# Windowed attention and a feed-forward block: the exponential moved behind the transposition of the scores

## The chip, the cores and the metric

The program runs on one core of a Trainium2 chip. Five engines of that core matter here. PE (TensorE) multiplies matrices into PSUM, PEld is its loading of weights, DVE (VectorE) and ACT (ScalarE) do elementwise work out of PSUM and SBUF, and SP issues the DMAs. POOL (GpSimd) does almost nothing. The metric is the device time of one execution in microseconds, and less is better.

## The reference

Two blocks follow each other. The first is attention with a window, for 8 batches, 8 heads, 512 local rows, 32 global rows and a head width of 64.

```
k_all = concat(k_g, k_l);  v_all = concat(v_g, v_l)
out_g = softmax(scale * q_g @ k_all.T) @ v_all          # 32 global rows see everything
s_ll  = where(|i - j| <= 32, scale * q_l @ k_l.T, -1e9) # local rows see a window ...
s_l   = concat(scale * q_l @ k_g.T, s_ll)               # ... and the global rows
out_l = softmax(s_l) @ v_all
softmax(s): e = exp(s - max(s)); e / (sum(e) + 1e-9)
```

The second is a feed-forward block on all 4352 rows, with 512 columns in, 2048 hidden and 512 out: `h = x @ w_in`, `g = h * erf(softplus(h))`, `out = g @ w_out`.

## The kernel before

**Attention.** A head is one batch and one of 8 heads, so there are 64 of them. Heads come in pairs. For a pair, `scores` writes two PSUM tiles `s` (128 rows of queries, 4 tiles of them, 128 keys each). For a head, `mask_max` (DVE, four custom instructions) copies the scores to the SBUF tile `sm`, adds the mask and keeps each row's maximum in `mx`. What follows depends on the head. In the first 30 heads in the program's counting (`biased`, `BIASED = 30`) the function `exps` runs four ACTIVATEs of 128x128 on ACT, each `exp(maximum - x)` with `mx` as its bias. In the other 34 heads DVE subtracts the maximum from the whole tile in one instruction of 128x512, and ACT takes the exponential of the whole tile in one more. Then, for every head, PE transposes `sm` into the PSUM tile `t`, ACT or DVE copies `t` to the SBUF tile `pt`, PE multiplies `pt` with the values (`o`), and DVE or ACT divides by the row sum (`xn`). The sum of a row comes with the values, as a column of ones.

**Global rows.** Sixteen groups of four heads do the same for the 32 global rows. Their scores are the PSUM tiles `ga` and `gb`, the maximum is `gn`, ACT takes the exponential from PSUM into the SBUF tile `pg`, PE transposes `pg` in two halves, and ACT or DVE copies each half to `gt`. Of `pg` some columns stand between the written ones and are set once, to zero.

**Feed-forward.** Its work is laid between the heads from the start on. Products are written as three matmuls of high and low parts (`wh` and `wl`, `xh` and `xl`), `h` and `pa` to `pd` are the first product, `op` is the second. `gate` is one uninterrupted block on ACT, for up to three hidden tiles at a time while attention lasts: a table load for softplus, the softplus of the tiles, a table load for erf, the erf of the tiles, and a table load that brings the exponential back.

**Order.** Nothing is scheduled at run time. Each step is an `Op`, made by `add`, with the engines that may do it. The long string `ORDER` lists every step's number in the order in which the instructions are issued to the engines' queues, and an `a` behind a number says that ACT takes a step which DVE could do as well. A `w` in it is a filler: a matmul on constants into a spare bank. Each engine executes its queue in order, and a semaphore makes an instruction wait for the data and for free buffers. All DMAs are issued by SP, in the order of the string too. PSUM has 6 banks for attention and the second product, and 2 for `h`.

Most instructions pass through helpers, so their lines are the helpers' own: L374 is a matmul, L375 a transposition on PE, L376 an ACTIVATE, L377 a table load, L378 a DMA, L386 any DVE or POOL instruction.

Of the kernel before, what the change touches and what calls it, by code (L numbers as in the profile page):

```python
# [25 lines left out]
NENT = 24  # L26
MASK = -8.0e9
# [10 lines left out]
STEP, GKEY = 0.093, -1.339  # L38
# [99 lines left out]
w w w w w w w w w 4 349 w 348 352 314 315 316 2 321 0 3 363 1 317 318 377 364 404 376 53 353 354 323 322 324 444 445  # L138
334 335 55 446 325 361 59 336 380 326 54 337 327a 405 447 448 56 57a 381 449 450a 332 61 58 319 320 459 460 461 462
451 382 338a 29 350 487 391 31 383 452a 453 454 328 384a 329 330 333 339 340 60 392 463 379 5 30 355 356a 362 331 341  # L140
342a 32 33 408 409 419 455a 393 394a 343 344a 62 365 366a 345 432 351 389 346a 486 35 456 63 457a 458 6 378 390 410
420 367 368 64 357 358 359 34 435 436 360 437 417 464 465a 476 369 370 510 511 421 385 512 513 477 422a 466 467a 514
478 479a 395 37 433 386 406 499 438 549 396 387 388a 7 371 372a 439a 373 474 418 374a 397 407 489 468 490 36 398a 411
412a 517 38 515 516a 469 w 518a 470a 399 400a 500 501 525 434 39 40 423 552 401 8 424 402a 553 413 471 414 415 1364
472a 498 9a 10 554 416 425 426 440 441 442 551 563 11 475 488 41 491 473 443a 573 574 555 575 576 550 492 427 556a 577
428a 493a 13 430a 519 480 481 528 564 494 429 482 580 611 527 537 529 530 1365 483 495 578 539 502 496 520 42 12 588
620 503a 565 566a 1366a 521a 579a 497 43 375 484 1361 14 540 15 557 558 581a 504 44 505 559 560 506 522 523a 485 1362
526 16 45a 46 507a 541 542a 614 615 616 591 598 599 634 538 561 635 636 562 17 531 592 47 1363a 649 508 637 621 19
1355 1356 532a 509 638 622 18 543 533 534 582 589 1357a 567 48 623 590 600 583 535 536 1358 568 569 132 624a 596 570
601a 593 672 597 20 639 571 572 640a 619 617 1359 618a 49 612 1413 1360a 613 584a 544 594 595 652 545 546 659 1373 21  # L150
641 50 1370 642 585 586 587 547 548 653 695 696 654 602 643 603 606 644 604 1414 1367 605 645 733 697 607 608 698 699
660 1415 1371 675 682 683 646 647a 1416 710 655 656 651 700 676 673 347 702 1374 701a 703a 680 661 662 657 1368 658
625 1417 1418 736 756 1372a 51 1421 650 609 626 22 1377 627 1380 1375a 629 1378 1369a 677 737 757 610 1376 248 758
1419 1383 1422a 743 744 628 630 631 632 1387 65 1384 742 704 663 705 681 678 679a 706 1425 759 760 664 665 666a 648 52
66 1390 67 1426a 761 738 667 762a 713 714 684 633 720 735 68 707 708a 1427 715 794 739 716 797 1379 69a 668 669 23 70
403 25 670 685a 674 686 771 1420a 717a 431 687 690 24 763 688 721 1428a 718 689a 691 692a 740a 1423 712 26 798 27a 805
83 799 764 28 722 723a 806 807 774 775 819 820 1385a 745 800 741 746 1391a 821 709 822 823 719 1429 781 77 80 711 734
765 106 671 71 693 1388a 1424a 1381a 1386 766 767a 859 724 779 747 782 1382 748 749 750a 725 726 727 1389 795 801 524
# [177 lines left out]
def kernel(  # L336
# [120 lines left out]
    def attention(b, h, key):  # L457
# [37 lines left out]
        load(key - VLEAD, VB, vB[b, h], 333)  # L495
        st["va", h % 4] = VA

        biased = NH * b + h < BIASED
        if h % 2 == 0:
            st["s"] = SS = [psum_a([P, 4, P], f"s_{nm}_{i}") for i in range(2)]  # L500

# [1043 lines left out]
```

## Time and profile before

| what | value |
|---|---|
| median of 3 runs | 889.73 us |
| lowest and highest run | 883.45 and 890.32 us |
| the profiled execution's own time | 886.39 us |
| its span, first to last instruction | 884.6 us |
| granted TensorE clock, mean | 0.998 |
| PE busy | 865.7 us, 98% of the span |
| DVE busy | 685.2 us, 77% |
| ACT busy | 566.7 us, 64% |
| DMA queue of the program | 185.02 MB, 64.9% of 16 engines' span |

The span lies 1.8 us below that execution's own time. The shares of busy time are averages over a program whose stages differ: attention with feed-forward work between the heads until about 325 us, then feed-forward work alone. So the same numbers are taken by stretches further down. The ends of matmuls are modelled, so a busy PE says that matmuls follow each other, and the time from one start to the next says how fast.

### The profile page before, as it was taken

The page shows a single profiled execution, that of the slowest core. Times are in us where ns is not written, and L with a number is a line of the kernel's source. Part 1 is how long each engine was busy: PE and PEld are TensorE (multiplying, and loading weights), DVE is VectorE, ACT ScalarE, POOL GpSimd, SP SyncE. Part 2 cuts the span into 40 slices and gives each one's busy share as a digit, 9 for nine tenths or more (in the row PEclk, how much of TensorE's full clock was granted, in tenths as well). Part 3 has the DMA queues.
Part 4 walks back from the last instruction along what each step waited for, and adds up shares of the span by engine and source line. Part 5 has one row for each costly group of instructions (what it writes and reads, how often), then busy time and mean ns, then how long its engine had stood idle before and what let it go on. Part 6 is the DMA issues. An engine that isn't in the chain of part 4 may idle for free.

```text
span 884.6 us, 22103 instructions
## 1 busy us (share of the span) xinstructions
PE 865.7 (98%) x8752; PEld 711.6 (80%) x8753; DVE 685.2 (77%) x1810; ACT 566.7 (64%) x1025; POOL 0.9 (0%) x5
## 2 busy tenths in 40 slices
PE   6899999999999999999999999999999999999998
PEld 4678787888888888888888888888888888888986
DVE  5989998999998989899988977496647956355443
ACT  6989989766766866775746845565644653465660
POOL 0000000000000000000000000000000000000000
PEclk9999999999999999999999999999999999999999
DMA  9889998988788766887776529343573536335212
GB/s 331 298 276 322 311 293 294 308 271 279 253 267 267 237 219 200 282 284 256 233 243 206 175 83 328 101 131 120 156 248 96 163 101 193 117 112 149 86 69 71
DMA packets 120062, 186.42 MB, mean 211 GB/s; under 512 B 14104, under 2 KB 57624, under 8 KB 119960
## 3 DMA queue, kind: packets, MB, share of 16 engines
q1 hardware_dynamic: 119960, 185.02, 64.9%
q8 instruction: 69, 1.13, 0.5%
q14 instruction: 33, 0.27, 0.1%
HBM read 143.56 MB, written 41.42 MB: 209 GB/s over the span
## 4 chain that ended last, share of the span: by engine, by line
PE 90%; DVE 4%; DMA 4%; ACT 1%; issue 1%; SPq 0%; DVEq 0%
PE op L374 40%; PE h L374 11%; PE pd L374 7%; PE pa L374 7%; PE pc L374 7%; PE pb L374 4%; PE o L374 3%; PE s L374 3%; PE t L375 3%; PE h_g L374 2%; PE go L374 1%; PE ga L374 1%; PE gt L375 1%; DVE sm L386 1%; DMA raw_in<-in_w_in_dram 1%; DVE top_in L386 1%
## 5 line engine op out<-in xcount | busy, mean ns | idle before, releaser
L374 PE MATMUL op<-wouth,gh 128*128 128x512 f32 x544 | 214.7, 395 | 0.1
L374 PE MATMUL op<-wouth,gl 128*128 128x512 f32 x544 | 212.0, 390 | 0.0
L374 PE MATMUL op<-woutl,gh 128*128 128x512 f32 x544 | 211.8, 389 | 0.0
L377 ACT ACT_TABLE_LOAD x105 | 134.7, 1283 | 2.5 <-PEq L1532 0.7
L374 PEld LDWEIGHTS op<-wouth,gl 128*128 128x128 f32 x544 | 102.1, 188 | 21.5
L374 PEld LDWEIGHTS op<-wouth,gh 128*128 128x128 f32 x544 | 102.2, 188 | 20.5 <-ACT xg L376 0.3
L374 PEld LDWEIGHTS op<-woutl,gh 128*128 128x128 f32 x544 | 102.3, 188 | 20.0
L376 ACT ACTIVATE gh<-sp 128x512 fp32r<-128x512 f32 x75 | 46.9, 629 | 96.2 <-PE op L374 87.3
L386 DVE TENSOR_TENSOR gl<-sp,gh 128x512 fp32r<-128x512 f32 x136 | 91.7, 687 | 20.3 <-PE op L374 16.0
L376 ACT ACTIVATE sp<-sp 128x512 f32<-128x512 f32 x136 | 76.0, 621 | 0.5
L386 DVE CUSTOM_DVE_ANT_0 sm<-s,msk 128x128 f32<-128x128 f32 x256 | 58.3, 285 | 14.0 <-ACT msk L376 7.0
L374 PE MATMUL h<-xh,winh 128*128 128x512 f32 (+1 forms) x168 | 66.4, 395 | 0.0
L386 DVE CAST gh<-sp 128x512 fp32r<-128x512 f32 x61 | 25.6, 420 | 50.6 <-PE op L374 50.3
L374 PE MATMUL pa<-xh_x_B,wq 128*128 128x512 f32 x184 | 64.1, 389 | 0.0
L374 PE MATMUL pd<-xh_ih_T,wq 128*128 128x512 f32 x184 | 64.0, 389 | 0.0
L374 PE MATMUL h<-xh,winl 128*128 128x512 f32 (+1 forms) x168 | 63.3, 377 | 0.0
L374 PE MATMUL h<-xl,winh 128*128 128x512 f32 (+1 forms) x168 | 63.0, 375 | 0.0
L386 DVE TENSOR_TENSOR pair<-u,pc 128x512 f32<-128x512 f32 x46 | 31.4, 684 | 25.3 <-PE pc L374 25.1
L374 PEld LDWEIGHTS pd<-xh_ih_T,wq 128*128 128x128 f32 x184 | 34.5, 188 | 7.5 <-ACT abs_l_in L376 0.2
L374 PEld LDWEIGHTS pa<-xh_x_B,wq 128*128 128x128 f32 x184 | 34.5, 188 | 7.2
L375 PE MATMUL t<-cs,sm 128*128 128x128 f32 x256 | 39.1, 279 | 0.5 <-DVE mx L386 0.5
L376 ACT ACTIVATE sm<-sm,mx 128x128 f32<-128x128 f32 x120 | 37.6, 399 | 2.8 <-DVE mx L386 2.8
(158 smaller groups left out, 1685.7 us busy)
## 6 DMA issues: line engine op xcount, KB each, us to landing
wq<-wq SPq DMA_DIRECT2D x161, 256.0 KB, 3.5
vb<-in_vB_dram SPq DMA_DIRECT2D x64, 325.0 KB, 5.3
qk<-in_qk_dram SPq DMA_DIRECT2D x28, 656.0 KB, 6.2
rx<-xsc SPq DMA_DIRECT2D x26, 512.0 KB, 6.5
va<-in_vA_dram SPq DMA_DIRECT2D x64, 195.0 KB, 4.8
wq<-part SPq DMA_DIRECT2D x47, 256.0 KB, 4.0
part<-os SPq DMA_DIRECT2D x34, 256.0 KB, 3.8
os<-part SPq DMA_DIRECT2D x34, 256.0 KB, 3.9
```

What stands on the lines that cost most here:

```text
L374: pe = lambda n, *a, **k: pinned(nc.tensor.matmul(n, *a, **k))
L375: tr = lambda *a, **k: pinned(nc.tensor.transpose(*a, **k))
L376: act = lambda *a, **k: pinned(nc.scalar.activation(*a, **k))
L377: table = lambda name: pinned(nc.scalar.preload_act_table_set(name))
L386: return lambda *a, **k: pinned(f(*a, **k))
```

## The change

The exponential leaves its place ahead of the transposition. Ahead of it only the maximum is subtracted, on DVE (one instruction of 128x512) or on ACT (four of 128x128, with the function Identity), as `ORDER` says for each head. The copy of the transposed tile out of PSUM becomes the exponential, so it is now always on ACT. The global rows are treated in the same way, and the untouched columns of `pg` are set to -1e30 in place of zero, so that their exponential is zero. `mx` has 6 buffers in place of 2. `ORDER` is another list.

```diff
@@ ORDER is another list of step numbers; its first line before:
-w w w w w w w w w 4 349 w 348 352 314 315 316 2 321 0 3 363 1 317 318 377 364 404 376 53 353 354 323 322 324 444 445
...
-    add({"POOL": 0.7}, -99, lambda: pool.memset(PG.ap, 0.0), writes=[PG])
+    add({"POOL": 0.7}, -99, lambda: pool.memset(PG.ap, LOWEST), writes=[PG])
...
-        MX = abuf([P, 4], f"mx_{nm}", "mx", 2)
+        MX = abuf([P, 4], f"mx_{nm}", "mx", 6)
...
         def mask_max(ts=range(4)):
+            biased = shift.eng == "ACT"
...
-        def exps():
+        def subtract(e):
+            if e == "DVE":
+                dve.tensor_tensor(SM.ap, SM.ap, MX.ap.unsqueeze(2).to_broadcast([P, 4, P]), ALU.subtract)
+                return
             for t in range(4):
-                act(SM.ap[:, t, :], SM.ap[:, t, :], AF.Exp, bias=MX.ap[:, t : t + 1], scale=-1.0)
+                act(SM.ap[:, t, :], SM.ap[:, t, :], AF.Identity, bias=MX.ap[:, t : t + 1], scale=-1.0)
...
-        if biased:
-            add({"ACT": 1.18}, key, exps, [TAB, MX] + ([PIECE[3, h]] if NH * b + h < 2 else []), [SM])
-        else:
-            add({"DVE": 0.62, "POOL": 1.13},
-                key,
-                lambda e: vec[e].tensor_tensor(
-                    SM.ap, SM.ap, MX.ap.unsqueeze(2).to_broadcast([P, 4, P]), ALU.subtract
-                ),
-                [MX],
-                [SM],
-            )
-            add({"ACT": 0.55}, key, lambda: act(SM.ap, SM.ap, AF.Exp, scale=scale), [TAB], [SM])
+            shift = add({"DVE": 0.62, "ACT": 1.18}, key, subtract, [MX], [SM])
...
-        add({"ACT": 0.52, "DVE": 0.61}, key + STEP * 2, lambda e: copy(e, PT.ap, T.ap), [T], [PT])
+        add(
+            {"ACT": 0.55},
+            key + STEP * 2,
+            lambda: act(PT.ap, T.ap, AF.Exp, scale=scale if shift.eng == "DVE" else 1.0),
+            [T, TAB],
+            [PT],
+        )
...
-            act(body, GA.ap.rearrange("p (m x) -> p m x", x=96), AF.Exp, bias=NM.ap, scale=scale)
-            act(PG.ap[:, 672:736], GB.ap, AF.Exp, bias=NM.ap, scale=scale)
-
-        add({"ACT": 0.8}, key, exps, [GA, GB, NM, TAB], [PG])
+            for dst, src in ((body, GA.ap.rearrange("p (m x) -> p m x", x=96)), (PG.ap[:, 672:736], GB.ap)):
+                if e == "DVE":
+                    dve.tensor_scalar(dst, src, scale, NM.ap, op0=ALU.mult, op1=ALU.add)
+                else:
+                    act(dst, src, AF.Identity, bias=NM.ap, scale=scale)
+
+        add({"DVE": 0.74, "ACT": 0.8}, key, subtract, [GA, GB, NM], [PG])
...
-                {"ACT": 0.42, "DVE": 0.48},
+                {"ACT": 0.44},
                 key + STEP * 2,
-                lambda e, T=T, m0=m0: copy(e, GT.ap[:, m0 : m0 + 3, :], T.ap),
-                [T],
+                lambda T=T, m0=m0: act(GT.ap[:, m0 : m0 + 3, :], T.ap, AF.Exp),
+                [T, TAB],
                 [GT],
```

Counted over the whole program, the change moves instructions as follows. The 34 ACTIVATEs of 128x512 on `sm` are gone. The ACTIVATEs of 128x128 on `sm` go from 120 to 156 (30 heads to 39), the DVE subtractions from 34 to 25. Writing `pt` goes from 50 on ACT and 14 on DVE to 64 on ACT, writing `gt` from 24 on ACT and 8 on DVE to 32 on ACT. Writing `pg` goes from 16 groups on ACT to 9 on ACT and 7 on DVE. Table loads stay at 105. Among the first 30 heads, counted by batch and head, six have the subtraction on DVE after the change (none before), and five had their `pt` written by DVE before (none after). Fillers go from 11 to 4: ten of the 11 stand ahead of PE's first score, and the 4 stand in the first batches' heads.

What ACT issues around the end of batch 4 and the start of batch 5 before, where each head's number follows its tile (`sm_4_7` is batch 4, head 7):

```order
L376 ACTIVATE sm_5_3_3899<-sm_5_3_3899 128x512
L376 ACTIVATE sm_4_7_3612<-sm_4_7_3612 128x512
L376 ACTIVATE pg_78<-ga_5_0_3947,gn_5_0_4007 128x5x96
L376 ACTIVATE pg_78<-gb_5_0_3948,gn_5_0_4007 128x64
L376 ACTIVATE sm_5_0_3986<-sm_5_0_3986 128x512
L376 ACTIVATE pt_4_7_4059<-t_4_7_4058 128x512
L376 ACTIVATE os_0_1_1_4070<-op_0_1_1_3973 128x512
L376 ACTIVATE part_3_2_4075<-top_l_in_3_1_3798 128x256
L376 ACTIVATE hs_0_2_3_4113<-h_0_2_3_3811 128x512
L376 ACTIVATE os_0_1_0_4168<-op_0_1_0_4077 128x512
L376 ACTIVATE part_3_5_4172<-top_l_in_3_0_3387 128x256
L376 ACTIVATE pt_5_0_4096<-t_5_0_4095 128x512
```

What ACT issues there in the changed kernel:

```order
L375 ACTIVATE sm_5_0_3828<-sm_5_0_3828,mx_5_0_3829 128x128 x4
L375 ACTIVATE gh_0_1_5_3926<-sp_0_1_5_3282 128x512
L376 ACT_TABLE_LOAD
L375 ACTIVATE sp_0_2_0_4006<-hs_0_2_0_3582 128x512
L375 ACTIVATE sp_0_2_1_4007<-hs_0_2_1_3542 128x512
L375 ACTIVATE sp_0_2_2_4008<-hs_0_2_2_3594 128x512
L376 ACT_TABLE_LOAD
L375 ACTIVATE sp_0_2_0_4006<-sp_0_2_0_4006 128x512
L375 ACTIVATE sp_0_2_1_4007<-sp_0_2_1_4007 128x512
L375 ACTIVATE sp_0_2_2_4008<-sp_0_2_2_4008 128x512
L376 ACT_TABLE_LOAD
L375 ACTIVATE pt_5_0_4028<-t_5_0_4027 128x512
```

Before, head 5_0 passes ACT twice, for its exponential (`sm_5_0`) and for the write of `pt_5_0`. In the changed kernel it passes ACT for the subtraction and then for the write of `pt_5_0`, which is the exponential; between the two stands a whole gate block, whose last instruction brings back the table for the exponential.

What DVE issues at the start before, from the `mask_max` of the last of the first four heads on, where `top_in` is the conversion of a tile of weights and `gm`, `gn` are maxima of the global rows:

```order
L386 ISA sm_0_1_245,mx_0_1_246<-s_0_0_1_161,msk_76 128x128
L386 ISA mx_0_1_246 128x1
L386 TENSOR_SCALAR top_in_0_2_0_251<-raw_in_0_2_0_199 128x512
L386 SCALAR_TENSOR_TENSOR top_in_0_2_0_251<-raw_in_0_2_0_199,top_in_0_2_0_251 128x512 x2
L386 TENSOR_REDUCE gm_0_0_243<-gb_0_0_234 128x1
L386 TENSOR_SCALAR gn_0_0_319<-gm_0_0_243 128x1
L386 SCALAR_TENSOR_TENSOR top_in_0_2_0_251<-winh_0_2_308,top_in_0_2_0_251 128x512
L386 ISA sm_0_4_325,mx_0_4_326<-s_0_4_0_268,msk_76 128x128
L386 ISA mx_0_4_326 128x1
```

What DVE issues first of all in the changed kernel:

```order
L385 TENSOR_SCALAR top_in_0_2_0_117<-raw_in_0_2_0_106 128x512
L385 SCALAR_TENSOR_TENSOR top_in_0_2_0_117<-raw_in_0_2_0_106,top_in_0_2_0_117 128x512 x2
L385 SCALAR_TENSOR_TENSOR top_in_0_2_0_117<-winh_0_2_111,top_in_0_2_0_117 128x512
L385 ISA sm_0_2_185,mx_0_2_186<-s_0_2_0_151,msk_76 128x128
L385 ISA mx_0_2_186 128x1
```

The conversion of the first tile of weights (four instructions on `top_in_0_2_0`) moves from behind the `mask_max` of four heads to the very start.

What SP issues first before, where `q` and `k` are queries and keys of a pair of heads (`0_2` is batch 0, heads 2 and 3), `mby` is the mask and `raw_in` a tile of weights:

```order
L378 DMA k_0_2_116<-in_qk_dram 128x768
L378 DMA q_0_2_119<-in_qk_dram 128x544
L378 DMA q_0_0_155<-in_qk_dram 128x288
L378 DMA k_0_0_156<-in_qk_dram 128x416
L378 DMA mby_77<-in_cst_dram 128x128
L378 DMA cs_75<-in_cst_dram 128x194
L378 DMA q_0_0_155<-in_qk_dram 128x256
L378 DMA k_0_0_156<-in_qk_dram 128x352
L378 DMA k_0_4_189<-in_qk_dram 128x768
L378 DMA q_0_6_195<-in_qk_dram 128x544
L378 DMA q_0_4_197<-in_qk_dram 128x544
L378 DMA raw_in_0_2_0_199<-in_w_in_dram 128x512
```

What SP issues first in the changed kernel:

```order
L377 DMA raw_in_0_2_0_106<-in_w_in_dram 128x512
L377 DMA k_0_0_110<-in_qk_dram 128x416
L377 DMA q_0_2_114<-in_qk_dram 128x544
L377 DMA mby_77<-in_cst_dram 128x128
L377 DMA q_0_0_109<-in_qk_dram 128x288
L377 DMA k_0_2_125<-in_qk_dram 128x768
L377 DMA cs_75<-in_cst_dram 128x194
L377 DMA k_0_0_110<-in_qk_dram 128x352
L377 DMA vb_0_1_129<-in_vB_dram 128x650
L377 DMA va_0_6_131<-in_vA_dram 128x390
L377 DMA q_0_0_109<-in_qk_dram 128x256
L377 DMA k_0_4_226<-in_qk_dram 128x768
```

The weights go from the 12th place to the first, the mask stays about where it is, the second half of `q_0_0` goes from 7th to 11th, and the keys of the pair 0_2 from 1st to 6th.

## Rows read from the trace of the kernel before

**Rows 1.** The page: the span, and PE's busy time, share and instructions.

```profile
span 884.6 us, 22103 instructions
PE 865.7 (98%) x8752; PEld 711.6 (80%) x8753; DVE 685.2 (77%) x1810; ACT 566.7 (64%) x1025; POOL 0.9 (0%) x5
```

**Rows 2.** Busy us of each engine by stretches, granted clock, DMA share, GB/s.

```profile
0.00:5.00 5.00, 4.23 (x14) 1.38 (x14) 0.00 (x0) 1.28 (x1) 0.94 (x5) 1.00 0.65 193
5.00:18.00 13.00, 6.55 (x228) 4.54 (x231) 8.15 (x48) 8.45 (x24) 0.00 (x0) 1.00 1.01 363
18.00:22.00 4.00, 4.00 (x91) 3.24 (x87) 3.91 (x15) 3.71 (x11) 0.00 (x0) 0.57 1.06 395
22.00:110.00 88.00, 80.50 (x1985) 63.50 (x1975) 80.40 (x348) 79.86 (x209) 0.00 (x0) 1.00 0.90 301
110.00:143.00 33.00, 32.90 (x693) 27.05 (x693) 30.06 (x100) 28.88 (x64) 0.00 (x0) 1.00 0.97 322
143.00:331.00 188.00, 187.70 (x3270) 153.24 (x3259) 173.09 (x627) 134.97 (x262) 0.00 (x0) 1.00 0.81 260
331.00:862.00 531.00, 531.00 (x2434) 443.43 (x2433) 382.59 (x663) 308.95 (x459) 0.00 (x0) 1.00 0.55 172
...
```

**Rows 3.** PE's waits, longest first: what waited, for whom, us, times, longest.

```profile
PE s L374 <- issue: 2.8, 2, 2.0
PE s L374 <- DVE mx L386: 2.4, 1, 2.4
PE gt L375 <- ACT pg L376: 2.1, 1, 2.1
PE s L374 <- DMA q<-in_qk_dram: 1.9, 1, 1.9
PE ga L374 <- DMA qk<-in_qk_dram: 1.6, 1, 1.6
...
```

**Rows 4.** PE's waits from 143 us to the end, all of them.

```profile
PE t L375 <- DVE mx L386: 0.3, 1, 0.3
```

**Rows 5.** Instructions on `sm`: ns min/median/max, first and last start, shapes.

```profile
L376 ACT ACTIVATE sm<-sm,mx x120: 384/394/453, 7.4 to 129.7; 128x128 f32<-128x128 f32 x120
L386 DVE TENSOR_TENSOR sm<-sm,mx x34: 650/685/694, 116.3 to 310.7; 128x512 f32<-128x512 f32 x34
L376 ACT ACTIVATE sm<-sm x34: 613/630/720, 118.7 to 322.9; 128x512 f32<-128x512 f32 x34
```

**Rows 6.** Groups by line: busy us, mean ns of one | idle before.

```profile
L377 ACT ACT_TABLE_LOAD x105 | 134.7, 1283 | 2.5 <-PEq L1532 0.7
L376 ACT ACTIVATE sp<-sp 128x512 f32<-128x512 f32 x136 | 76.0, 621 | 0.5
...
L376 ACT ACTIVATE sm<-sm,mx 128x128 f32<-128x128 f32 x120 | 37.6, 399 | 2.8 <-DVE mx L386 2.8
L376 ACT ACTIVATE pt<-t 128x512 f32<-128x512 f32 x50 | 29.7, 602 | 10.3 <-PE t L375 10.3
...
L376 ACT ACTIVATE pg<-ga,gn 128x480 f32<-128x480 f32 x16 | 10.6, 661 | 8.9 <-DVE gn L386 8.0 <-PE go L374 0.9
...
L386 DVE TENSOR_REDUCE gm<-ga 128x1 f32<-128x480 f32 x16 | 10.4, 652 | 0.6 <-PE ga L374 0.6
...
L386 DVE COPY pt<-t 128x512 f32<-128x512 f32 x14 | 9.6, 684 | 0.3
```

**Rows 7.** The start, by time: start us, us, instruction, [idle before].

```profile
0.77 4.27 PE L374 MATMUL spare<-const-bfloat16-1.0 128*128 128x512 bf16 x10 [0.77 <-PEq L1532]
...
4.97 1.95 PE L374 MATMUL s<-k,q 64*32 64x128 f32 x96
...
6.37 0.63 ACT L376 ACTIVATE msk<-mby 128x512 f32<-128x512 uint8 x1 [4.36 <-DMA mby<-in_cst_dram]
...
13.94 0.43 DVE L386 TENSOR_SCALAR top_in<-raw_in 128x512 int32<-128x512 int32 x1 [1.62 <-DMA raw_in<-in_w_in_dram]
14.40 1.42 DVE L386 SCALAR_TENSOR_TENSOR top_in<-raw_in,top_in 128x512 int32<-128x512 int32 x2
```

More of the change, by code (lines that the diff above doesn't have):

```diff
@@ L26 @@
 NENT = 24
+LOWEST = -1.0e30
 MASK = -8.0e9
@@ L143 @@
[L143 to L152, printed above, removed]
@@ new lines @@
+2040a 2167 1731 1991 1994 1990 1732a 2041 2000 1997 1992 1733 1911 2001a 1998 1742 1735 1916 2168 1737 1921 1738 1739
+1926 2002 1741 1743 2169 2004 1999 2042 2003 1744 1748 2006 2020 2074 2082 2090 2008 2005 2007 1912 1745 2009 1747
+2188 2043 1917 1913a 2189 2172 2044a 1922 1914 1749 2173 1750a 1927 1751 2010 2045 2046 2012 2047a 2011 2190 1918a
+2048 2021 2013 2191 1919 2049 2023 2022 2192 2170 2027 2024 2193 2171 2025 2194 2098 2028 1752 2174 2029 2209 2026
+2175 2031 2210 2030 2179a 2195 2211 2050 2181a 2053 2033 2212 2051 2196a 2056 2054a 2052 2069 2213 2183a 2055 2059
@@ new lines @@
+2432 2153 2433 2161 2434 2287 2442 2301a 2289 2307 2440a 2467 2310 2304a 2313 2452 2468 2438a 2316 2288 2138 2453a
+2469 2290 2435 2146 2140 2291 2148 2439 2141 2326 2443a 2470 2149 2292 2441 2154 2444 2334 2331 2156 2162 2302 2339
+2305 2157 2342 2308 2319 2164 2309 2454 2311 2165 2312 2350 2455 2471 2347 2456 2314 2315 2317 2458 2355 2457a 2320
+2472 2318 2327 2323 2487 2358 2335 2343 2351 2460 2321 2322 2324 2473 2488 2325 2359 2328 2474a 2489 2362 2365 2336
+2459 2368 2344 2461 2462 2464 2463 2490 2352 2465 2491 2475 2360 2363a 2361 2477 2364 2492 2476 2371 2479 2478 2493
@@ L263 @@
+3004 2904 3012 3005 3013 3007 2916 3015 3008 2924 3016 2932 2909 2917 2911 2925 2919 2912 2933 2927 2920 2935 2928
+2937 2936 2938
 """
@@ L564, in attention @@
             add({"DVE": 0.44}, key + 0.001, lambda: mask_max(range(2, 4)), [S, MSK, PIECE[2, 0], SM, MX], [PIECE.setdefault((3, h), fixed(None))])
+            shift = add({"DVE": 0.62, "ACT": 1.18}, key, subtract, [MX, PIECE[3, h]], [SM])
         else:
             add({"DVE": 0.86}, key, mask_max, [S, MSK], [SM, MX])
-        if biased:
-            add({"ACT": 1.18}, key, exps, [TAB, MX] + ([PIECE[3, h]] if NH * b + h < 2 else []), [SM])
-        else:
-            add({"DVE": 0.62, "POOL": 1.13},
-                key,
-                lambda e: vec[e].tensor_tensor(
-                    SM.ap, SM.ap, MX.ap.unsqueeze(2).to_broadcast([P, 4, P]), ALU.subtract
-                ),
-                [MX],
-                [SM],
-            )
-            add({"ACT": 0.55}, key, lambda: act(SM.ap, SM.ap, AF.Exp, scale=scale), [TAB], [SM])
+            shift = add({"DVE": 0.62, "ACT": 1.18}, key, subtract, [MX], [SM])
         T = psum_a([P, 4, P], f"t_{nm}")
```

228 lines of the change are left out of this document (112 added, 116 removed).

## The prediction

> **What bounds the kernel now.** I read the page's busy shares first, then the table of stretches, then PE's waits, then single groups. PE is busy for 865.7 of 884.6 us [rows 1], which leaves 18.9 us of idle time in the whole span. The reader is to see where it lies [rows 2]. From 143 to 862 us PE idles for 0.3 us (188.0 less 187.7, then 531.0 of 531.0), and its list of waits from 143 us to the end has one entry of 0.3 us [rows 4]. That its busy time there is real work is seen in the rate: 2434 matmuls in 531 us are one in 0.218 us, nearly all of 512 columns, which is the higher clock level of 2.4 GHz with little between them. Nothing that ACT or DVE saves there can end sooner, unless PE gets fewer instructions, and this change gives it none fewer but fillers. The idle time is early: 6.45 us in 5 to 18 us (13.00 less 6.55), 7.5 us in 22 to 110 us, 0.1 us in 110 to 143 us. In that early part all are loaded: from 22 to 110 us DVE is busy for 80.4, ACT for 79.9 of 88 us, and the DMA engines at 0.90 [rows 2]. The longest waits of PE there have five different causes [rows 3].
>
> **The removed pass.** The 34 heads that passed both DVE and ACT ahead of the transposition, and then ACT or DVE once more, lose one pass. Their instructions start at 116.3 us at the earliest and go on to 322.9 us [rows 5]. On ACT, 34 of 0.630 us go (-21.4). The 36 more pieces of 128x128 cost 37.6/120 = 0.313 us each of busy time (+11.3), the 14 more writes of `pt` cost 29.7/50 = 0.594 (+8.3), and the 7 fewer writes of `pg` save 10.6/16 = 0.66 (-4.6) [rows 5, 6]. That is -6.4 us. On DVE 9 subtractions of 0.685 (-6.2) and 14 copies of 9.6/14 = 0.686 (-9.6) go. The 7 writes of `pg` come: no row shows that instruction, the nearest is the maximum over the same PSUM tile, 0.65 us (+4.6) [rows 5, 6]. That is -11.2 us. In all some 17.6 us of two engines, nearly all behind 116 us, where the work that hides it is PE's own: PE idled 0.4 us from 110 to 331 us. **Worth: 0 us** (at best -0.4).
>
> **The other heads.** In the first 30 heads nothing is removed. Four ACTIVATEs of 128x128 with `mx` as bias stay four of that shape and bias, with another function. The copy out of PSUM becomes an exponential out of PSUM. No row has one of 128x512. Its bounds are the copy from PSUM (0.594 us) and the exponential from SBUF (0.630), 0.04 us apart, or 2.3 us of ACT over 64 heads. I take the copy's, since both read PSUM. What differs early is who does it. Six subtractions go from ACT (4 x 0.313 = 1.25) to DVE (0.685): ACT -7.5, DVE +4.1. Five writes of `pt` go from DVE to ACT: DVE -3.4, ACT +3.0. Three of the first seven `pg` go to DVE: ACT -2.0, DVE +2.0. So ACT gets 6.5 us less and DVE 2.7 us more, on some 110 us. Of the 7.5 us that PE idles in 22 to 110 us, 2.8 are charged to "issue" and 1.6 to the DMA of `qk` [rows 3], neither of which the change touches. The other 3.1 us are waits on ACT or DVE. The ends are -3.1 us (all gone) and +2.7 us (DVE's added work passed on to PE whole). I take **-1.0 us**, a third of the gain, since ACT is relieved by more than DVE is loaded, but DVE is the fuller of the two.
>
> **The start.** Rows give the pace of the loads. PE's first scores start at 4.97 us, once 384 + 272 KB are in (a column of 128 rows is 0.5 KB), and the mask's conversion at 6.37 us, 416 KB later [rows 7]. That is 297 KB per us. In the new order of SP the mask is behind 1056 KB in place of 1072, so no later. But the keys for the first `mask_max` now end at 1584 KB, 4.97 + 928/297 = 8.1 us. Their 64 matmuls take 1.3 us (96 took 1.95), so DVE's first `mask_max` starts near 9.4 in place of 7.0 us (+2.4). Against this DVE has the conversion of weights done by then, 0.43 + 1.42 + half of 1.42 for the last = 2.6 us (-2.6), which formerly came at 13.94 us after a wait of 1.62 us for its load, and that wait goes (-1.6). A new wait comes: the second half of `q_0_0` is 11th in SP's queue, at 2505 KB, 4.97 + 1849/297 = 11.2 us. With its scores done at 11.8 us, DVE waits for about 0.6 us from 11.2, when two heads' worth at 0.9 are done (+0.6). In sum **-1.2 us**, between -6.4 (PE's waits of 2.4, 2.1 and 1.9 us all gone) and +2.4 (the later scores felt in full).
>
> **The fillers.** Ten stood in the wait for the first load, so their 4.27 us [rows 7] are worth nothing by themselves. What they do is seen by the clock: each took 427 ns for 512 columns, the level of 1.2 GHz, and the scores behind them ran at the level of 2.4 (granted 1.00 from 5 to 18 us). Then, after 13 us in which PE was busy for only 6.55, the granted clock was 0.57 in 18 to 22 us [rows 2], which cost 4.0 x 0.43 = 1.7 us of work. Without fillers PE enters the first scores cold. The ends are 0 (the lower level lies in the waits, 6.45 us of them from 5 to 18 us) and +6.5 us (all of the 6.55 us of work takes twice as long, and nothing hides it). I take **+1.7 us**, the price of the one stretch at the lower level that the trace has. The Trainium skill, page "TensorE: Matmul & The Clock Gate", section "What's actually happening", says that the throttled clock is the default and that activity releases it, which speaks against taking the fillers out; by it alone the sum would be nearer the upper end, 890.7 us. The trace agrees, with 427 ns in the first fillers and 0.57 after the idle stretch. The four fillers that stand later cost 0.218 us each at most (+0.9); they stand among the first batches' heads, where PE idles anyway, so I count 0.
>
> **The sum.** 886.39 us, the profiled execution's own time, -1.2 - 1.0 + 1.7 = **885.9 us**. That execution lies 3.3 us below the median of 889.73 and inside the runs' 883.45 to 890.32. So 885.9 may be seen as no change, and the next median may as well lie some 3 us to either side of it. About 1% is what a measurement of this kernel tells from no change: 880.8 and 898.6 us.
>
> **Rivals.**
> *Faster: the early idle time closes.* The new list of steps is free to rearrange everything, and ACT has 6.5 us less to do before 116 us. Should PE's 7.5 us of 22 to 110 us and the stretch at the lower clock (1.7) both go, the time is 886.4 - 9.2 = 877.2 us. For it speaks that DVE and ACT are at 91% there, so that little relief shortens queues. Against it: "issue" and the DMA hold 4.4 us of it, the DMA engines are at 0.90 to 1.06 until 143 us, and DVE gets more, not less. Chance 0.15.
> *Cold start.* The lower clock lasts through the first scores and is not hidden: +6.5 - 1.2 - 1.0 on 886.4, or 890.7 us, up to 893 if the start's gain fails too. For: the fillers are gone. Against: idle time of nearly the same size to hide it. Chance 0.12.
> *Slower: the exponential sits behind a gate block.* Only ACT can now empty the bank `t`. A block is three table loads of 1.283 us and six passes of 76.0/136 = 0.559 us, 7.2 us [rows 6], uninterrupted, and the order on ACT shows one right between the subtraction and the exponential of head 5_0. Where PE's queue has less than 7.2 us of other work between a head's transpositions and its values, PE waits with everything behind it, in the stretch that has no waits now. It decides from two blocks on (of 105/3 = 35) that catch PE for their whole length: 886.4 + 14.4 = 900.8 us. Against: 50 of 64 writes of `pt` were on ACT already, behind the same blocks, and PE waited 0.3 us in all from 143 us on [rows 4]. Chance 0.07.
>
> **How the numbers follow.** The forecast, no change, has 0.66, and its own range is 881 to 891 us: the ends of the early heads (-3.1, +2.7) and of the start, not all on one side, and the runs' scatter. The range that should hold 8 in 10 reaches into the cold start (893) and into the faster case (879). Left out are two thirds of the faster case, 0.10, the gate blocks, 0.07, and 0.03 of the rest. Faster by over 1% (under 880.8 us): 0.13, nearly all of the faster case. Slower by over 1%: 0.07, the gate blocks. Within 1%: 0.80.
>
> **What would show it.** The removed pass: ACT's 34 instructions of 128x512 on `sm` are gone, DVE's busy share of 143 to 331 us falls from 173.1 us by about 10, and PE's idle time there stays under 1 us. The early heads: PE's idle time of 22 to 110 us stays between 5 and 10 us. The start: DVE's first instruction is the conversion at about 4.5 us, its first `mask_max` comes at 9 to 10 us. The fillers: the clock shows a longer stretch at the lower level before 25 us. Gate blocks: a wait of PE's `o` on ACT's `pt` of several us. I am wrong if PE idles for more than 20 or less than 7 us behind 5 us, or if its matmuls of 331 to 862 us take another time each, for which I know no reason.

## The result: 1.1% slower, nearly all of it lost before 331 us

The changed kernel takes 899.4 us (median of 6 runs, 893.17 to 901.11) beside 889.73 us for the kernel before (6 runs, 883.45 to 891.05), a ratio of 1.0110 [1.0075, 1.0145]. Measured once more later, it came to 898.63 us and 1.0129 [1.0085, 1.0172]. That is not the "no change" of the forecast. The profiled execution took 901.11 us with a span of 899.3. It is the slowest of its six, and that of the kernel before (886.39 us) lies below its median, so the two traces are 14.7 us apart and the medians 9.7.

The page of the changed kernel, to be read beside [rows 1]: PE is busy for 871.4 us. Before it was 865.7, or 861.4 without the ten fillers at the start, so 10.0 us more go into the same work and three more late fillers, and 4.7 us more into idle time (27.9 in place of 18.9 + 4.3).

```profile
span 899.3 us, 22044 instructions
...
PE 871.4 (97%) x8743; PEld 717.2 (80%) x8746; DVE 679.5 (76%) x1804; ACT 560.9 (62%) x1019; POOL 0.9 (0%) x5
```

The table of stretches of the changed kernel, with the columns of [rows 2]:

```profile
0.00:5.00 5.00, 0.00 (x0) 0.00 (x0) 0.96 (x2) 1.96 (x2) 0.94 (x5) 1.00 0.63 214
5.00:18.00 13.00, 9.15 (x217) 6.34 (x218) 6.90 (x40) 4.32 (x12) 0.00 (x0) 1.00 1.02 363
18.00:22.00 4.00, 3.99 (x93) 3.06 (x94) 3.93 (x20) 3.92 (x12) 0.00 (x0) 1.00 1.00 317
22.00:110.00 88.00, 75.78 (x1780) 60.57 (x1780) 73.30 (x316) 67.28 (x177) 0.00 (x0) 0.92 0.80 260
110.00:143.00 33.00, 32.52 (x676) 27.03 (x673) 31.65 (x120) 29.19 (x67) 0.00 (x0) 1.00 0.91 297
143.00:331.00 188.00, 185.50 (x3245) 149.57 (x3245) 162.56 (x604) 135.44 (x279) 0.00 (x0) 1.00 0.83 273
331.00:862.00 531.00, 531.00 (x2604) 443.22 (x2604) 386.05 (x684) 309.18 (x462) 0.00 (x0) 1.00 0.56 177
```

From 331 to 862 us PE idles in neither kernel, at the full clock. In 22 to 110 us PE idles 12.2 us (7.5 before), at a granted clock of 0.92 (1.00 before): the trace has the level of 1.2 GHz from 25.7 to 35.9 and from 56.4 to 59.8 us. In 143 to 331 us PE idles 2.5 us (0.3 before). DVE and ACT are less busy in 22 to 110 us, not more, by 7.1 and 12.6 us, so neither holds PE up there by having more to do.

PE's waits in the changed kernel, longest first, as in [rows 3]:

```profile
PE s L373 <- DMA q<-in_qk_dram: 7.9, 2, 7.6
PE s L373 <- issue: 5.0, 3, 3.4
PE o L373 <- issue: 4.0, 2, 2.5
PE gx L373 <- DVE rs L385: 1.7, 1, 1.7
PE t L374 <- ACT gt L375: 1.2, 1, 1.2
PE o L373 <- ACT pg L375: 1.0, 1, 1.0
```

The first row is the start: no fillers fill the wait, and the first queries and keys come later (7.59 us in place of 4.97). The next two are the news: 9.0 us charged to "issue", that is to nothing that the profile shows. Before, the only such row on the list is 2.8 us [rows 3]. No wait on ACT's `pt` is among the longest.

A sum over time shows when the loss comes. Each matmul is counted with the mean step that its kind (tile and shape) took in the trace of before, and the work done so far is taken from the time. The difference of the two kernels, an estimate good to some 0.5 us:

```
us from the start      18    30    60    80   143   260   331   862
lost, after - before   1.0   3.3   7.1  10.0   9.9  13.0  14.2  14.9
```

The start of the changed kernel, as in [rows 7]:

```profile
4.00 0.43 DVE L385 TENSOR_SCALAR top_in<-raw_in 128x512 int32<-128x512 int32 x1 [4.00 <-DMA raw_in<-in_w_in_dram]
...
7.10 0.63 ACT L375 ACTIVATE msk<-mby 128x512 f32<-128x512 uint8 x1 [2.42 <-DMA mby<-in_cst_dram]
7.59 2.91 PE L373 MATMUL s<-k,q 64*32 64x128 f32 x96 [7.59 <-DMA q<-in_qk_dram]
...
10.64 0.29 DVE L385 CUSTOM_DVE_ANT_0 sm<-s,msk 128x128 f32<-128x128 f32 x1 [3.94 <-PE s L373]
```

The 96 matmuls of the first scores take 2.91 us in place of 1.95, so PE does enter cold. The trace has no record of the granted clock before 15.4 us (4.8 us in the kernel before), so the 1.00 in the table for 5 to 18 us holds for the last 2.6 us of it only. Yet by 18 us only some 1.0 us has been lost against the kernel before.

The groups that the change touches, as in [rows 5, 6]:

```profile
L375 ACT ACTIVATE sm<-sm,mx 128x128 f32<-128x128 f32 x156 | 49.5, 398 | 14.8 <-DVE mx L385 14.8
L375 ACT ACTIVATE pt<-t 128x512 f32<-128x512 f32 x64 | 37.6, 600 | 18.0 <-PE t L374 17.9
...
L385 DVE TENSOR_SCALAR pg<-ga,gn 128x480 f32<-128x480 f32 x7 | 5.0, 717 | 0.4
```

The exponential out of PSUM takes 600 ns, as the copy did (602). Every instruction that the prediction priced has that price, within 0.07 us.

### The profile page after: what moved, and what is told of

Read it like the earlier page. It is cut to its first block, busy times and chain, and to the rows that moved or that the text cites. A ratio compares the mean times of both kernels' runs of the same rounds, so it can differ in the third digit from the quotient of the medians.

```text
span 899.3 us, 22044 instructions
## 1 busy us (share of the span) xinstructions
PE 871.4 (97%) x8743; PEld 717.2 (80%) x8746; DVE 679.5 (76%) x1804; ACT 560.9 (62%) x1019; POOL 0.9 (0%) x5
## 4 chain that ended last, share of the span: by engine, by line
PE 93%; DMA 3%; ACT 1%; issue 1%; DVE 1%; SPq 0%; DVEq 0%; ACTq 0%
PE op L373 41%; PE h L373 11%; PE pc L373 7%; PE pa L373 7%; PE pd L373 7%; PE s L373 4%; PE o L373 4%; PE pb L373 3%; PE t L374 3%; DMA vb<-in_vB_dram 2%; PE h_g L373 2%; PE ga L373 1%; PE gt L374 1%; PE go L373 1%; DMA q<-in_qk_dram 1%
## 5 line engine op out<-in xcount | busy, mean ns | idle before, releaser
L375 ACT ACTIVATE sm<-sm,mx 128x128 f32<-128x128 f32 x156 | 49.5, 398 | 14.8 <-DVE mx L385 14.8
L375 ACT ACTIVATE pt<-t 128x512 f32<-128x512 f32 x64 | 37.6, 600 | 18.0 <-PE t L374 17.9
L373 PE MATMUL o<-va,pt 128*32 128x65 f32 x768 | 38.4, 224 | 3.4 <-issue 1.5
```

Source lines behind the costliest of these rows:

```text
L373: pe = lambda n, *a, **k: pinned(nc.tensor.matmul(n, *a, **k))
L375: act = lambda *a, **k: pinned(nc.scalar.activation(*a, **k))
```

## What a stop charged to "issue" is

The rows about the longest of them, by time, PE in the changed kernel:

```profile
51.27 1.06 PE L373 MATMUL s<-qk 64*32 64x128 f32 x51
...
55.77 0.33 PE L373 MATMUL s<-qk 64*32 64x128 f32 x7 [3.44 <-issue]
```

PE stops in the middle of one step, whose inputs its first 51 matmuls have already used. Of the queues of DMA there are two besides the program's that carry something then (from 52.4 to 55.7 us):

```profile
q8 instruction: 1, 0.02, 1.7%
q14 instruction: 1, 0.01, 0.6%
```

The first of them moves 69 packets of 16 KB in the whole span, for the 17,489 matmuls and loads of weights of the page and 253 semaphore instructions among them: one packet for about 256 instructions of PE. The other has 33 packets of 8 KB in the span, too few for PE. In the 20 traces of this case, PE stopped 51 times for more than 1.0 us (behind 18 us) at the same place of its instruction stream, the 190th to 195th of 256 counted from the start with the semaphores (a trace can lack a few records, which moves the count by some three), and went on 2.4 us (median, 2.2 at least) after the last packet of the first queue had begun. The other 36 stops of that length lie at any place. So PE had run out of instructions. Packets that come in time leave no trace in PE's row. The stop at 52 us has a run of short matmuls ahead of it: the 192 instructions before it took 1.6 us, as long as seven matmuls of 512 columns at 0.218. The other stops are like it. PE passed that place 1342 times behind 18 us in the 20 traces, and 333 times it had taken under 5 us for the 232 instructions before. 49 of the 51 stops are among those 333, two among the other 1009.

The Trainium skill, page "Runtime: NRT & Kernel Launch", section "Instruction fetch mechanics", says that an engine's instructions are fetched in blocks of 16 KiB, 256 instructions, while it executes, and that crossing a block's end is mostly hidden. The size agrees with the packets here. "Mostly hidden" holds for most crossings here (51 stops of over 1.0 us in 1342) but doesn't make them free: the stops at that place sum to 2.0 us before, 8.7 us after (7.3 in a second trace), and to 27.1 us in the worst run below.

## The experiments

All were timed beside the kernel before; each ratio is to it. A step's number in the lists is that of `ORDER`.

### The list and the arithmetic apart

**e1.** The new arithmetic in the old list: each step at the place where it was, the 34 passes left out, all `pt` and `gt` by ACT.

```diff
-w w w w w w w w w w 53 0 314 54 316 348 2 55 3 315 56 57a 349 1 318 333 ...
+w w w w w w w w w 4 349 w 348 352 314 315 316 2 321 0a 3a 363 1 317 318 377 ...
```

> The whole change of the arithmetic (subtraction ahead of the transposition, exponential out of PSUM on ACT), but every step in the place that it has in the old list; each head's subtraction on the engine that it or the exponential had there, the 34 removed exponentials dropped, all writes of pt and gt on ACT. Theory A (the loss is the new list's first 90 us: PE starved and at the lower clock): within 0.5% of before, 884 to 891 us, PE idle from 22 to 110 us near 7.5 us, one stretch at half clock. Rival B (the loss is the moved exponential itself: ACT alone empties the bank): 895 to 902 us, with waits of o for pt on ACT. Rival C (the gain and loss cancel: the arithmetic wins and the list loses): under 882 us.

900.82 us, 1.0113 [1.0079, 1.0147]: Rival B by its number; what waits on ACT behind 60 us is `go` on `gt` and `gx` on `pt`, not `o` on `pt`. The new list by itself is not needed for a loss.

**e2** and **e3.** Hybrids: the order of the one list up to the eighth step of the first product, then that of the other, both with the new arithmetic. e2 starts as the old list, e3 as the new.

```diff
+old list's words up to its 8th h step, then the new list's words that are left   (e2)
+new list's words up to its 8th h step, then the old list's words that are left   (e3)
```

> The changed kernel, with the old list up to the eighth group of the first product (about 76 us of the trace of before), and the remaining steps in the new list's order. Theory A: most of the 14.7 us is back, 885 to 892 us; no stretch at half clock over 4 us. Rival D (the loss is spread over the new list up to 300 us): 893 to 898 us. Rival B: about 899 us.

> The changed kernel, with the new list up to the eighth group of the first product, and the remaining steps in the old list's order: the mirror of the run before. Theory A: 896 to 901 us, half clock for over 10 us around 26 to 36 us. Rival D: 890 to 895 us. Rival B: about 899 us too, so it is told apart by the other two.

e2 898.59 us, 1.0119 [1.0082, 1.0157]; e3 913.5 us, 1.0245 [1.0192, 1.0299]. e2 fits Rival B and lies just over D's range, A's is far; no theory had e3. If each half of a list had a cost of its own, e2 and e3 together would cost what e1 and the changed kernel do together, 2.2%, and not 3.6%. But where the lists are joined the hybrids make waits of their own, 5.3 us on DVE's `mx` at 79 us in e2 and 5.9 us on ACT's `pt` at 93 us in e3, so they settle little. What e2 and e3 also change, and no theory then allowed for, is where every PE instruction stands in its block.

### Who copies, and behind what

**e6.** The exponential follows the transposition only in the 50 heads whose copy was ACT's already.

```diff
+        late = nm not in COPIED
...
-                act(SM.ap[:, t, :], SM.ap[:, t, :], AF.Exp, bias=...
+                act(SM.ap[:, t, :], SM.ap[:, t, :], AF.Identity if late else AF.Exp, bias=...
...
+            if not late:
                 add({"ACT": 0.55}, key, lambda: act(SM.ap, SM.ap, AF.Exp, scale=scale), [TAB], [SM])
...
+        if late:
+            power = 1.0 if biased else scale
+            add({"ACT": 0.55}, key + STEP * 2, lambda: act(PT.ap, T.ap, AF.Exp, scale=power), [T, TAB], [PT])
```

> The kernel before with its list. The exponential follows the transposition only in the 50 heads whose tile ACT copied out of PSUM anyway; the 14 heads whose copy is DVE's and all global rows keep the exponential where it was. Theory A (the cost of the arithmetic in the old list comes from copies that move from DVE to ACT and there stand behind gate blocks, and from the global rows): 885 to 891 us. Rival B (the exponential out of PSUM costs PE time by itself, wherever it stands): 896 to 902 us, as with the whole new arithmetic in the old list, 900.8.

`COPIED` names the 14 heads whose tile DVE copies. 890.5 us, 1.0022 [0.9991, 1.0052]: Theory A. The moved exponential costs no more than 0.5%. No gain shows either, though 25 passes of 0.630 us are gone from ACT.

**e7.** Only the copies: the kernel before, with the 14 `pt` and 8 `gt` of DVE given to ACT.

```diff
-... 1360a 613 584a 544 594 595 652 545 ...
+... 1360a 613 584a 544 594 595a 652 545 ...
```

> The kernel before with its arithmetic and its list, but the 14 copies to pt and the 8 copies to gt that DVE did are ACT's, at the same places of the list. Theory A (copies behind gate blocks make PE wait; ACT also has 12 us more to do): 896 to 904 us, with waits of PE on ACT's pt or gt of several us in the trace. Rival B (who copies is without effect, the moved exponential is what costs): 887 to 891 us.

901.33 us, 1.0156 [1.0113, 1.0199]: Theory A, with no exponential moved. PE's waits from 60 us on in e7:

```profile
PE go L374 <- ACT gt L376: 2.9, 1, 2.9
PE gx L374 <- ACT pt L376: 2.2, 1, 2.2
PE o L374 <- issue: 2.2, 1, 2.2
```

And ACT by time around the second of them:

```profile
148.23 1.28 ACT L377 ACT_TABLE_LOAD   x1
149.52 1.67 ACT L376 ACTIVATE sp<-sp 128x512 f32<-128x512 f32 x3
151.21 1.28 ACT L377 ACT_TABLE_LOAD   x1
152.50 0.60 ACT L376 ACTIVATE pt<-t 128x512 f32<-128x512 f32 x1
```

This tile `t` (head 3_5) was ready at 147.1 us. The copy stands behind a gate block and starts when its last table load ends, 5.4 us later. DVE, in the kernel before, took it 0.7 us after it was ready. The third row is no fetch, since it lies at the 93rd place of its block: DVE stands still for 2.4 us there, waiting for `sp` out of a gate block, and PE goes on 0.1 us after DVE, behind that, has read the `o` tiles.

**e9.** e7 with the five copies that waited over 4 us behind a gate block given back to DVE.

```diff
-... 642a ... 784a ... 1102a ... 1150a ... 1232a ...
+... 642  ... 784  ... 1102  ... 1150  ... 1232  ...
```

> The kernel before with 17 of the 22 copies moved from DVE to ACT. The five that stay with DVE are those that waited over 4 us behind a gate block when ACT did all 22 and that DVE did at once: the second half of gt of batch 2, pt of heads 3_5, 6_0 and 7_0, the first half of gt of batch 6. Theory A (the place behind a gate block costs, not who copies nor ACT's load): 888 to 893 us, no wait of PE over 1.5 us behind 60 us. Rival B (ACT's 12 us more of work cost): 897 to 901 us, near the 901.3 of all 22.

894.28 us, 1.0071 [1.0038, 1.0103]: neither. Five of 22 copies hold 7 of the 13 us, so the place on ACT matters most, but the 17 others still cost something. This chain accounts for most of e1, whose waits from 60 us on are the same (3.4 on `gt`, 2.2 on `pt`, 2.2); a stop of 4.0 us at a block's end (51 us) is the longest of its others. It does not explain the changed kernel, whose list puts copies elsewhere: one wait of 1.2 us on `gt` at 257.6 us is all of it behind 143 us.

### Fillers

**e4.** The changed kernel with the ten fillers of before at its front.

```diff
-53 0 314 54 ...
+w w w w w w w w w w 53 0 314 54 ...
```

> The changed kernel with the ten fillers of before set back ahead of PE's first score, nothing else. If the cold start is what costs (the scores of 7.6 to 15.4 us at the lower level, and a clock that falls again at 25.7 us), then 892 to 895 us, and the first 96 matmuls of scores take 2.0 in place of 2.9 us. If the later starving costs (stops in the middle of groups of matmuls at 24 and 52 us, then half clock), then 897 to 900 us, with the stops where they were.

893.82 us, 1.0034 [0.9998, 1.0070]: cold start, by its number.

**e5.** The kernel before without its ten.

```diff
-w w w w w w w w w 4 349 w 348 352 ...
+4 349 348 352 ...
```

> The kernel before without the ten fillers that stand ahead of PE's first score, nothing else changed. Theory A (cold start: the fillers were worth about 5 us wherever they stand, since adding them to the changed kernel took it from 899.4 to 893.8 us): 893 to 896 us, first 96 matmuls of the scores near 2.9 us in place of 1.95. Rival B (the old list hides a cold start in its early waits; the fillers paid only with the new list): 887 to 891 us.

893.76 us, 1.0054 [1.0023, 1.0085]: cold start again. Both fit, and both were read wrongly, as e14 shows.

**e8**, **e11**, **e12.** More fillers, against the lower clock that follows early waits: 15 more than e4 in the changed kernel, 21 more in the kernel before, and e8 with another 15 between short steps near 50 us.

```diff
+w w w w w w 352 ... w w 444 ... w w 343 ... w w 456 ... w w w 471          (e8)
+w w w w w w w w 322 ... w w w w w w 380 ... w w w w w w w 449              (e11)
+e8, and w w w w w 528 ... w w w w w 573 ... w w w w w 552                  (e12)
```

> The changed kernel with its list, the ten fillers of before at its front, and 15 more ahead of the steps of PE that waited there in the run with the ten alone: six ahead of the second scores, two ahead of the first global scores, two each ahead of the first xn and gx, three ahead of the second gx. Theory A (what is left against the kernel before, 893.8 to 889.0 us, is the lower clock that follows PE's early waits): 888 to 892 us, with fewer stretches at the lower level. Rival B (what is left is waiting itself, and fillers take the places of work): 893 to 897 us.

> The kernel before with 21 more fillers in three early waits of PE: 8 ahead of the rest of the scores of heads 0 and 1, 6 ahead of the scores of heads 4 and 5, 7 ahead of the first transposition of pg. Theory A (the lower level of the clock after these waits, 3 to 5 us of work in a median run, can be saved): 884 to 887 us, a mean granted clock of 0.997 or more. Rival B (the lower level moves to later stops, or the fillers take the places of work): 888 to 892 us.

> The kernel with the list of the change, ten fillers at the front and 15 in early waits (893.6 us), and 15 more between the steps of short matmuls that follow each other near 50 us: five each ahead of the scores of heads 4 and 5 of batch 1, of the second global scores, and of the scores of heads 6 and 7. Theory A (PE stops there for 3.4 to 4.0 us because it uses up its instructions faster than they arrive): no stop over 1.5 us at these steps, 888 to 892 us. Rival B (the stop comes from something else and stays): a stop of 2 us or more there, 894 to 898 us.

e8 893.63 us, 1.0056 [1.0027, 1.0084]; e11 893.15 us, 1.0067 [1.0042, 1.0092]; e12 898.66 us, 1.0130 [1.0069, 1.0191]. e8 is Rival B; e11 and e12 are slower than either of their theories. The clock rose as meant, to a median of 0.998 in e11 and 0.999 in e12 (0.996 before), and the time with it. In e11 the stops at blocks' ends sum to 9.6 us. In e12 a stop of 2.3 us stayed, at the 194th place, with fillers now in front of it; 33 fillers more than before are also 7 us of PE at 0.218 each, of which the waits hide a part. A full clock does not make up for either.

### The place in the block alone

**e10.** The changed kernel unchanged, for a second trace.

> The changed kernel once more, for a second trace of it. Theory A (the stops of PE within a group of matmuls are chance in size, but in the list of the change there are more of them): 897 to 901 us, stops charged to issue of 5 to 9 us in sum, not all at the same steps. Rival B (they are fixed by the list): the same steps stop, near 24, 52, 78 and 168 us, each within 0.5 us of 2.5, 3.4, 1.5 and 1.3.

898.63 us: Theory A. Five stops at blocks' ends, 7.3 us; of the four in the first trace three come again (24, 74 and 164 us, of 1.9, 1.3 and 1.1 us); the longest, at 52 us, does not. Most of the places where PE runs dry come back, how long it stops varies.

**e13** and **e14** tell warming and place apart: pairs of instructions, a load of one column and a matmul of one column, that fill places in the queue and leave PE idle.

```diff
+    prog.tick = lambda: pe(spare[:1, :1], warm[:, :1], warm[:, :1], start=True, stop=True)
-53 0 314 54 ...
+n n n n n n n n n n 53 0 314 54 ... (the changed kernel's list, e13)
-w w w w w w w w w 4 349 w 348 352 ...
+n n n n n n n n n n 4 349 348 352 ... (e14)
```

> The changed kernel with ten pairs of instructions at the front of PE's queue that do almost nothing (a load of one column of weights and a matmul of one column). They move every later instruction of PE by 20 places, as the ten fillers of the run at 893.8 us did, but keep PE idle. Theory A (the fillers were worth 5.6 us because they warm the clock): 897 to 900 us. Rival B (they were worth it because they moved PE's instructions against the blocks of 256 in which they are fetched): 892 to 895 us.

> The kernel before with its ten fillers at the front replaced by ten such pairs that do almost nothing, so that PE enters the first scores cold but every instruction has the place in the queue that it had. Theory A (cold start): 892 to 895 us, as without the fillers (893.8). Rival B (place in the queue): 887 to 890 us.

e13 895.21 us, 1.0057 [1.0021, 1.0094]: just over Rival B's range. e14 889.27 us, 0.9989 [0.9969, 1.0010]: Rival B. PE in e14, by time:

```profile
4.71 2.82 PE L377 MATMUL s<-k,q 64*32 64x128 f32 x96 [3.55 <-DMA q<-in_qk_dram]
```

The first scores run cold, 2.82 us in place of 1.95, and the kernel is as fast as before. The 0.5% of e5 was the 20 places. That goes by the medians; the two traces, of executions of 888.27 us (e5) and 889.32 us (e14), have stops at blocks' ends of 5.5 and 4.6 us and don't show the difference.

**e15.** The kernel before, with 59 such pairs ahead of its other work.

```diff
+w w w w w w w w w w n n n n n n n n n n 4 349 348 352 ... n (49 times) 322 ...
```

> The kernel before with its fillers and 59 pairs that do almost nothing (ten behind the fillers, 49 ahead of the rest of the scores of heads 0 and 1, where PE waits 2.4 us), so that all later instructions of PE stand 118 places further on. Theory A (PE stops where a block of 256 instructions ends in a dense run of short matmuls; worked out from the trace of before, that place would then fall into such runs near 24, 29, 41, 45, 55, 66, 237 and 314 us, some 7 us of stops more in sum, and stretches at the lower clock behind some): 894 to 900 us, with stops charged to issue at the 190th to 194th instruction of a block, two or three of them behind 200 us. Rival B (the place in the queue is without effect): 887 to 891 us, no stop over 0.5 us behind 143 us.

917.9 us, 1.0293 [1.0236, 1.0350]: the mechanism of Theory A at three times its size, far over its range. PE's waits behind 18 us and the stretches, e15:

```profile
PE o L378 <- issue: 15.6, 6, 3.8
PE h L378 <- issue: 8.3, 6, 2.6
PE s L378 <- issue: 2.8, 1, 2.8
```

```profile
22.00:110.00 88.00, 72.25 (x1734) 56.78 (x1735) 70.77 (x307) 70.01 (x181) 0.00 (x0) 0.93 0.80 266
110.00:143.00 33.00, 28.85 (x627) 23.40 (x626) 26.57 (x108) 24.13 (x66) 0.00 (x0) 0.97 0.84 265
143.00:331.00 188.00, 177.07 (x2929) 143.81 (x2929) 158.32 (x562) 126.49 (x246) 0.00 (x0) 0.98 0.78 250
```

Eleven stops of over 1.0 us at the 193rd to 195th place, 27.1 us, from 24 to 367 us. Five of them are at five of the eight places named beforehand: in the trace of before these places lay at 24, 41, 55, 66 and 237 us, and with the stops ahead of them they come at 24.0, 43.0, 57.3, 74.0 and 262 us. The other three that were named had no stop of over 1.0 us, and six stops came at places that were not named. Behind six of the eleven (24, 57, 74, 106, 139, 262 us) the granted clock falls to half for 3.4 us. No arithmetic, no order and no wait of the work was changed.

**e16** and **e18.** The changed kernel at a place worked out to be good, 44 instructions further on, with ten fillers (e16) and without (e18).

```diff
+w w w w w w w w w w n n n n n n n n n n n n  (then the changed kernel's list, e16)
+n n n n n n n n n n n n n n n n n n n n n n  (then the changed kernel's list, e18)
```

> The changed kernel with the ten fillers of before and twelve pairs that do almost nothing at the front, so that PE's later instructions stand 44 places further on. From the traces so far (how long PE takes for the 232 instructions ahead of each block's 193rd, against the delays of the fetches there) this is among the places with the fewest stops for this list, 20 places further on is near it. Theory A (most of the 1.1% is the place): 890 to 893 us. Rival B (with the ten pairs or fillers all that can be had is had, and 4 to 5 us come from copies that only ACT can do): 893 to 896 us.

> The changed kernel with 22 pairs that do almost nothing at the front and no fillers there, so that PE's instructions have the places of e16 (890.6 us) but PE enters the first scores cold. Theory A (the place is all of the 1.1%, the warming nothing): 890 to 892 us. Rival B (half of the gain of e16 was the warm start, as 893.8 with ten fillers beside 895.2 with ten such pairs lets one suspect): 893 to 896 us.

e16 890.57 us, 1.0012 [0.9985, 1.0039]: Theory A. e18 892.09 us, 1.0047 [1.0020, 1.0074]: nearer Theory A, a little over its range. The stretches of e16:

```profile
22.00:110.00 88.00, 82.89 (x2022) 65.02 (x2010) 81.89 (x349) 77.09 (x194) 0.00 (x0) 1.00 0.91 303
...
143.00:331.00 188.00, 186.77 (x3138) 150.99 (x3137) 166.44 (x603) 133.76 (x280) 0.00 (x0) 1.00 0.81 267
```

With one stop of 1.4 us at a block's end PE idles 5.1 us in 22 to 110 us, at full clock. What stays behind 143 us is the wait of 1.2 us on `gt`.

**e17.** e6 with one step of `h`, long matmuls, put ahead of the values and scores in which PE stops near 52 us in seven traces that begin with the old list (before, e1, e2, e5, e6, e7, e14; in e9 it waits only 0.4 us there). Step 429 moves ahead with it.

```diff
-... 428a 493a 13 430a 519 480 481 528 564 494 429 482 580 ... 539 1340 ...
+... 428a 429 493a 13 430a 519 1340 480 481 528 564 494 482 580 ... 539 ...
```

> The kernel of e6 (exponential behind the transposition where ACT copied anyway, 890.5 us beside 888.3) with one step of the first product, six long matmuls, put ahead of the values and scores in which PE stops near 52 us in every kernel with the old list. Theory A (the stop of 1.8 to 3.4 us there comes from the run of short matmuls ahead of the block's end): no stop over 1 us there, 886 to 889 us. Rival B (the fetch is late for other reasons): the stop stays at 1.8 us or more, 889 to 892 us.

886.4 us, 0.9975 [0.9954, 0.9997]: Theory A. PE's waits behind 18 us in e17:

```profile
PE ga L374 <- DMA qk<-in_qk_dram: 1.7, 1, 1.7
PE gb L374 <- issue: 1.1, 1, 1.1
```

The stop of 1.8 us in e6 is gone, one of 1.1 us at 48 us is left. It is the only kernel here whose interval lies below the one before; with an interval that ends at 0.9997, among 18 that were timed, a quarter of a percent is as much as can be said.

## Why the prediction was wrong

**The step that failed** is in the part on the other heads: of PE's idle time it put 2.8 us down to "issue", "neither of which the change touches". The change does touch it. A new list and fewer fillers put every PE instruction at another place of its block, and the stops went from 2.0 to 8.7 us, with 13.7 us at half the clock in 22 to 110 us in place of none. Idle time at stops (6.7 us more) and half clock (13.7 us of it in place of the 3.4 at 18 us, so up to 5.1 us more of lost work) make up some 11 to 12 of the 14.7 us between the traces. e15 shows that place alone can do this, e13 and e18 that moving the changed kernel's instructions back and forth, with nothing else, takes it from 1.011 or 1.013 to 1.0057 and 1.0047.

**The fillers.** "Worth nothing by themselves" was true of their 4.27 us and missed that they hold 20 places. The price of the cold start, +1.7 us, is borne out in size, but the runs don't tell it from nothing: by the ratios 2 us between e4 and e13, 3 between e16 and e18, -1 between e14 and the kernel before, each with an uncertainty of some 3. The sign named for it showed in part: PE stays cold to 15.4 us, but the stretch at half clock of 18 to 22 us is gone, and the next one comes at 25.7 us, behind the stop at 24 us. The rival *Cold start* (890.7, up to 893) comes near e5's 893.8, but e14 shows that its mechanism is not what cost there.

**The other heads, -1.0 us:** PE idled 12.2 us in 22 to 110 us, over the 5 to 10 that were forecast. Three stops at blocks' ends hold 7.5 us of it (2.0 before), its waits on ACT and DVE 3.4 us (3.1 before by the prediction's count). So the gain did not come, the term lies within its ends, and the row that it set aside is what broke the forecast.

**The removed pass, 0 us:** not contradicted. e6 takes 25 of 34 passes away and ACT is busy for 123.6 us in place of 135.0 in 143 to 331 us, at 1.0022 [0.9991, 1.0052]. DVE fell there from 173.1 to 162.6 us in the changed kernel, as forecast (by about 10). PE's idle time there, forecast under 1 us, is 2.5: a fetch of 1.3 at 168.6 us and a wait of 1.2 on `gt`. The sums of this part left out the eight writes of `gt` (ACT +3.9 us, DVE -4.4) and the second, 64 columns wide, instruction of the seven `pg` (ACT -2.1, DVE +1.9); with neither engine at the limit there, this changes nothing.

**The start, -1.2 us:** the conversion came at 4.00 us (forecast 4.5), the first `mask_max` at 10.64 (forecast 9 to 10), since its scores began at 7.59 and ran cold. By 18 us the difference is some 1.0 us, the cold scores included, inside the range from -6.4 to +2.4.

**Gate blocks,** the rival on the slower side: the mechanism is real. In the old list, with the copies on ACT, the time is 901.33 us (e7, 1.6%), near the 900.8 forecast, but not as forecast: not two whole blocks of 7.2 us, but PE's waits of 2.9, 2.2 and 2.2 us and what stands behind them. In the changed kernel's own list it is 1.2 us, so it was not what made that slower. That its number lies beside the measured 899.4 is chance.

**The sum.** With a good place for its instructions and the fillers, the changed kernel stands at 1.0012 [0.9985, 1.0039] (e16). The forecast of no change holds for the arithmetic and the list; it failed for the program as it stands, by its place in the queue, some 6 to 7 us of the 10 (from 1.011 or 1.013 to e18), and some 3 us more that e16's fillers take back and whose parts, warmth and chance, the intervals don't separate. The sign that was named for being wrong showed, but only just: behind 5 us PE idles 22.9 us (27.9 less the first 5.0), over the 20 named, and 19.1 us if the end from 862 us on is left out. It is a weak sign, because two thirds of the loss sit in PE's busy time, in slower matmuls, which it left out.

## What to carry to other kernels

Where one engine is full and its instructions are short, look at every stop charged to "issue" by its place in the instruction stream before giving it a cause; if stops share a place modulo 256, any edit that adds or takes away instructions ahead of them can move the time, whatever it was meant to do. An experiment that adds or removes instructions then needs a control with as many that do nothing (e14 overturned e5). Long matmuls ahead of such a place took the stop away in the one case tried (e17). And a copy given to an engine that runs long uninterrupted blocks must be placed against those blocks, by when its input is ready.

## What the runs showed of the hardware

- PE stops where a block of 256 of its instructions ends, 51 times for over 1.0 us in 20 traces, up to 4.0 us, and goes on 2.4 us (median) after the block's packet has begun. All but two of these stops follow 232 instructions that took PE under 5 us. 59 pairs of instructions that do almost nothing moved the time by 2.9%.
- Behind some of these stops the granted clock falls to half for 3.4 us: in e15 behind six of eleven, of 1.9 to 3.8 us, and not behind two others of 2.3 and 2.7 us.
- What holds a packet back before it begins is not seen in the rows. Whether it is the loads on the same DMA engines was not tried.
- 49 pairs that do almost nothing took 1.36 us at 7.34 us, 28 ns a pair, so places in the queue are cheap to fill.
